# Another fixed order of TensorE in an attention iteration of a fused attention and expert kernel

## The chip, the cores and the metric

One core of one Trainium2 chip runs the whole program. The metric is the device time of one execution in microseconds (us). Three executions of the kernel before took 1117.29, 1118.50 and 1119.31 us; their median, 1118.5 us, is the time that is forecast against.

## What is computed

```python
# attention: 4 batches x 8 heads, 576 tokens, 64 columns a head
scores = q @ k.T / 8 + cum[:, None] - cum[None, :]   # cum = cumsum(log(f)), causal mask
attn = softmax(scores); x = attn @ v
# expert layer 1: 2304 tokens x 512, 8 experts, the best one of each token
logits = x @ w_gate + modality_bias[modality_id]
out = gate * (relu(x @ w1[e]) @ w2[e])
# layer 2: a rational function between two dense products
y = (P(h) / Q(h)) @ w_out      with h = out @ w_in
```

The change is in the first part alone, where the attention runs and the gate's logits are made from its result.

## The kernel before

The 32 heads are worked on in 16 pairs. Iteration p of the loop over pairs holds steps of several pairs at once, as a software pipeline: it turns q and k of pair p+2, finds the row maxima of pair p+1, makes the scores of pair p, multiplies the scores of pairs p-2 and p-1 with their values and makes the logits of pair p-2. There are 18 iterations; all steps are present in iterations 2 to 13.

Every operation is first recorded, with the tiles that it reads and writes. A planner (`Rec.flush`, L222) then orders the instructions of each engine: from a cost of each operation it simulates the engines, and an engine that becomes free takes, of the operations that are ready, the one with the best key; if one alone is ready, it takes that. The order of TensorE in the attention is the exception. While `nc.chained` is set, each TensorE operation is tied behind the one recorded before it, so TensorE follows the order of recording. That order is written out by hand in the string `ORDER` (L1445), read two characters at a time in the loop at L1527:

- M0 to M3 (`maxes`, L718): the scores of pair p+1, a quarter at a time, into a pair of PSUM banks; VectorE reduces them to row maxima. M1 is reduced in two pieces (896 and 128 columns), M2 in one of 576, M3 in one of 640.
- S0 to S3 (`scores`, L759): the scores of pair p, a quarter at a time, into a pair of banks; ScalarE takes the exponential from there, and GpSimd makes the low half of it.
- V (`values`, L790): the next chunk of 12 or 14 matmuls of the product with v; the digit is only a name. A pair has seven chunks: three for its first three blocks of tokens, four for the last two. The last three chunks of pair p-2 are V5, V6 and V7 of iteration p; then v0 opens pair p-1, and V1 to V4 are its first four. All chunks write one single PSUM bank ("pv"). Behind V3 and V7 VectorE divides what stands there by the sums in three instructions (a small TENSOR_SCALAR, a RECIPROCAL, and a TENSOR_TENSOR into x) and so empties the bank.
- L0, L1 (`logits`, L910): L0 turns x of pair p-2 in five transposes (three read the first three blocks of tokens, two the last two) into a pair of banks; ScalarE and VectorE split it in two halves. L1 multiplies these with the gate's weights, into the single bank "x". The stores of x to DRAM are recorded with L0.
- T0, T1 (`parts`, L671): T0 turns 512 tokens of q and k of pair p+2 in eight transposes into a pair of banks. `split` (L689) empties it: a copy on ScalarE makes the high half, then a subtraction on VectorE the low half, 1024 columns each. T1 does the same for the last 64 tokens in two transposes, by the bank "x" and 128 columns.
- m0 (`turned`, L748): turns the maxima of pair p+1, by the bank "x"; VectorE reduces them, and two DMAs put them into the tile that S0 of the next iteration reads.

The pairs of banks are a ring of three, taken in the order of recording by M, S, L0 and T0. So each of them waits until what stood three places before it has been read. The order before gives this: L0 takes the pair of M1, T0 that of S1, M3 that of M2, S2 that of L0, S3 that of T0. The bank "x" goes round m0, T1, L1.

```python
ORDER = "M0V5S0V6M1V7S1M2L0v0V1T0M3V2S2m0V3T1S3L1V4"
for x, g in zip(ORDER[::2], ORDER[1::2]):
    if x == "M" and p + 1 < NP:
        at.maxes(p + 1, int(g))
```

Of the kernel before, what the change touches and what calls it, by code (L numbers as in the profile page):

```python
# [1441 lines left out]
RW = (4, 3, 3)  # L1442
TW = 8
NR = (2, 2, 2, 2, 2)
ORDER = "M0V5S0V6M1V7S1M2L0v0V1T0M3V2S2m0V3T1S3L1V4"  # L1445
UP = {'conv': -2110000.0, 'conv2': -3000.0, 'early': 0, 'unit': -7000.0}


def program(tc, q, k, v, f, moe_modality_id, moe_w_gate, moe_modality_bias, moe_w1, moe_w2, moe2_w_in, moe2_w_out, moe2_a, moe2_b, out):
    nc = Rec(tc.nc)  # L1450
    with tc.manual_schedule(), ExitStack() as pools, tc.tile_pool(name="dr", bufs=1, space=DRAM) as dr:
# [64 lines left out]
        for p in range(NP + 2):  # L1516
# [7 lines left out]
            if p + 2 < NP:  # L1524
                at.prep(p + 2)
                t = at.parts(p + 2)
            for x, g in zip(ORDER[::2], ORDER[1::2]):  # L1527
                if x == "M" and p + 1 < NP:
# [85 lines left out]
```

## Time and profile before

| | us |
|---|---|
| median of three runs | 1118.5 |
| the profiled execution | 1123.07 |
| span of its instructions | 1121.4 |
| mean granted TensorE clock | 0.956 |
| TensorE busy | 1003.1 |
| VectorE busy | 854.4 |
| ScalarE busy | 651.3 |
| GpSimd busy | 405.4 |

The profiled execution took 1.7 us more than its span, and 0.4% more than the median. In the trace PE is TensorE, DVE VectorE, ACT ScalarE, POOL GpSimd, and SP the engine that issues most DMAs. Nearly all operations go through one helper, so they carry its line, L155; the groups of M and S carry L713. A step is told by its tiles and shapes: `pair<-keep,y` is L0, `pair<-keep,prep` T0, `one<-keep,prep` T1, `one<-keep,at` m0, `one<-y` L1, `one<-at` and `one<-at,old` V, and `pair<-f32r` M or S. In square brackets stands the idle time of the engine ahead of a row, and what ended it.

### The profile page before, as it was taken

The numbers are of one execution on the slowest core, as the hardware profiler recorded it, in microseconds if no ns is written. First come the engines' busy times: TensorE is split into PE (matmuls) and PEld (weight loads), VectorE is DVE, ScalarE is ACT, GpSimd is POOL, SyncE is SP. The second block draws the span as 40 slices with busy tenths as digits, with TensorE's granted clock in tenths as the row PEclk, the third lists the DMA queues.
The fourth block names the chain that finished last, engine by engine and source line by source line (L and its number), as shares of the span: only waits on it lengthen the run. The fifth ranks groups of instructions, "written<-read, shape, count | busy, mean of one in ns | idle before, by whom it ended". The sixth has DMA issues, their size and how long they took to land.

```text
span 1121.4 us, 22693 instructions
## 1 busy us (share of the span) xinstructions
PE 1003.1 (89%) x8246; PEld 853.2 (76%) x8246; DVE 854.4 (76%) x1557; ACT 651.3 (58%) x1034; POOL 405.4 (36%) x353
## 2 busy tenths in 40 slices
PE   3689988898746799999999999999999999999995
PEld 2577777776634578879888898889878887888793
DVE  5775756758788896787869767949769969979685
ACT  1465554465545675656567466637658667676472
POOL 9576675676742431223122121212222223121131
PEclk9999998898758699999999999999999999999999
DMA  7663333211478887301151543445354454553400
GB/s 180 166 172 86 105 73 82 51 45 47 99 233 220 268 270 238 83 1 39 48 160 46 153 134 102 142 132 151 114 163 140 119 182 132 156 154 105 123 1 19
DMA packets 157376, 138.28 MB, mean 123 GB/s; under 512 B 73392, under 2 KB 115664, under 8 KB 157264
## 3 DMA queue, kind: packets, MB, share of 16 engines
q1 hardware_dynamic: 152288, 123.63, 39.1%
q0 software_dynamic: 4640, 13.13, 3.7%
q8 instruction: 64, 1.05, 0.4%
q14 instruction: 48, 0.39, 0.1%
q10 hardware_dynamic: 336, 0.08, 0.0%
HBM read 120.38 MB, written 16.33 MB: 122 GB/s over the span
## 4 chain that ended last, share of the span: by engine, by line
PE 50%; DVE 22%; DMA 9%; issue 9%; ACT 4%; POOL 2%; SPq 2%; DVEq 0%; POOLq 0%; ACTq 0%
PE pair L155 31%; PE one L155 13%; DVE y L155 12%; PE pair L713 6%; DMA b<-in_moe_w_dram 4%; DVE at L155 4%; DVE b L155 4%; ACT y L155 3%; DVE keep L155 2%; ACT b L155 1%; SPq L155 1%; DVE f32r L155 1%; POOL f32r L155 1%; POOL y L155 1%; DMA ys<-b 1%
## 5 line engine op out<-in xcount | busy, mean ns | idle before, releaser
L155 DVE TENSOR_TENSOR b<-b,b 128x512 fp32r<-128x512 f32 x272 | 200.5, 746 | 67.6 <-ACT b L155 36.4
L155 PE MATMUL pair<-b,b 128*128 128x256 f32 (+1 forms) x1032 | 234.8, 329 | 16.5 <-DVE b L155 10.2
L155 ACT CAST b<-b 128x512 fp32r<-128x512 f32 x272 | 165.1, 618 | 124.4 <-PE one L155 46.1
L155 POOL TENSOR_TENSOR y<-y,y 128x512 f32<-128x512 f32 x72 | 107.3, 1491 | 302.4 <-ACT y L155 284.0
L155 PEld LDWEIGHTS pair<-b,b 128*128 128x128 f32 x1032 | 174.1, 198 | 50.2 <-DVE b L155 19.0
L155 PE MATMUL one<-b,b 128*128 128x512 f32 x552 | 181.1, 404 | 5.1 <-DVE b L155 3.3
L713 PE MATMUL pair<-f32r 64*128 64x288 f32 (+4 forms) x1152 | 128.6, 343 | 16.5 <-ACT f32r L155 6.8
L155 ACT ACTIVATE y<-y,keep 128x512 f32<-128x512 f32 x144 | 109.3, 769 | 36.1 <-POOL y L155 29.1
L155 POOL TENSOR_TENSOR old<-old,at 128x960 f16<-128x960 f32 (+1 forms) x64 | 109.6, 1724 | 46.6 <-ACT at L155 46.3
L155 DVE SCALAR_TENSOR_TENSOR y<-y,keep,y 128x512 f32<-128x512 f32 x144 | 116.9, 822 | 7.9 <-ACT y L155 4.6
L713 PEld LDWEIGHTS pair<-f32r 64*128 64x128 f32 x1152 | 94.6, 204 | 25.3 <-ACT f32r L155 7.3
L155 PE MATMUL pair<-f32r,y 128*128 128x512 f32 x378 | 110.9, 397 | 1.7 <-DVE y L155 1.6
L155 PEld LDWEIGHTS one<-b,b 128*128 128x128 f32 x552 | 95.7, 188 | 21.9 <-DVE b L155 6.8
L155 PE MATMUL pair<-y,f32r 128*128 128x256 f32 x624 | 103.8, 283 | 1.8 <-DVE y L155 1.8
L155 PEld LDWEIGHTS pair<-y,f32r 128*128 128x128 f32 x624 | 91.7, 188 | 9.3 <-DVE y L155 3.4
L155 ACT ACTIVATE old<-pair,keep 128x960 f32<-128x960 f32 (+1 forms) x64 | 59.4, 928 | 66.9 <-PE pair L713 63.9
L155 DVE TENSOR_REDUCE at<-pair 128x2 f32<-128x576 f32 (+1 forms) x96 | 66.2, 707 | 34.8 <-PE pair L713 30.6
L155 PE MATMUL pair<-at,y 128*128 128x512 f32 x270 | 90.1, 410 | 1.7 <-DVE y L155 1.4
L155 ACT ACTIVATE y<-y 128x512 f32<-128x512 f32 x104 | 66.8, 643 | 31.0 <-DMA y<-in_moe_w_in_dram 23.9
L155 PEld LDWEIGHTS pair<-f32r,y 128*128 128x128 f32 x378 | 67.8, 188 | 16.2 <-DVE y L155 4.1
L155 POOL DMA_INDIRECT keep<-xnat,keep x32 | 34.4, 1075 | 120.3 <-PE pair L155 50.9
L155 ACT ACTIVATE y<-pair,keep 128x512 f32<-128x512 f32 x70 | 54.3, 776 | 25.0 <-DVE y L155 20.2
(140 smaller groups left out, 1872.9 us busy)
## 6 DMA issues: line engine op xcount, KB each, us to landing
b<-in_moe_w_dram SPq DMA_DIRECT2D x272, 256.0 KB
y<-in_moe_w_in_dram SPq DMA_DIRECT2D x16, 512.0 KB
y<-in_moe_w_out_dram SPq DMA_DIRECT2D x16, 512.0 KB
ys<-b SPq DMA_DIRECT2D x25, 257.0 KB
y<-ys SPq DMA_DIRECT2D x18, 257.0 KB
prep<-in_v_dram SPq DMA_DIRECT2D x4, 1152.0 KB
prep<-in_q_dram SPq DMA_DIRECT2D x32, 128.0 KB
prep<-in_v_dram SPq DMA_DIRECT2D x32, 128.0 KB
```

The lines of the kernel that those rows point to most:

```text
L155: fn = lambda: getattr(getattr(s.nc, eng), name)(*(x() for x in ra), **{n: x() for n, x in rk.items()})
L713: T.matmul(o, lhsT=w, rhs=x, start=st, stop=sp, skip_group_check=True)
```

## The change

One string is replaced. L0 moves from between M2 and V1 to between V2 and S2, and so behind T0 and M3; T1 moves from between V3 and S3 to directly behind T0; V3 now stands ahead of m0. Since the ring of bank pairs follows the order of recording, its users change too: T0 now takes the pair of M1, M3 that of S1, L0 that of M2, S2 that of T0, and S3 that of M3. The bank "x" now goes round T1, m0, L1. No operation is added or removed, and the planner makes the order of the other engines anew.

```diff
-ORDER = "M0V5S0V6M1V7S1M2L0v0V1T0M3V2S2m0V3T1S3L1V4"
+ORDER = "M0V5S0V6M1V7S1M2v0V1T0T1M3V2L0S2V3m0S3L1V4"
```

## Rows read from the trace of the kernel before

**Rows 1.** The profile page: busy time of the engines, share of the span, instructions.
```profile
PE 1003.1 (89%) x8246; PEld 853.2 (76%) x8246; DVE 854.4 (76%) x1557; ACT 651.3 (58%) x1034; POOL 405.4 (36%) x353
```

**Rows 2.** Windows, 20 us of attention: length, busy time and instructions by engine, clock, DMA.
```profile
100.00:120.00 20.00, 19.00 (x334) 16.31 (x332) 12.13 (x33) 10.90 (x13) 11.84 (x10) 1.00 0.42 108
```

**Rows 3.** Timeline of PE, end of M2 to the next M0: start, length, engine, operation.
```profile
104.33 0.23 PE L713 MATMUL pair<-at 64*128 64x64 bf16 x4
104.61 0.55 PE L155 MATMUL pair<-keep,y 128*128 128x128 f32 x3
105.81 0.53 PE L155 MATMUL pair<-keep,y 128*128 128x128 f32 x2 [0.66 <-DVE y L155]
106.28 0.23 PE L155 MATMUL one<-at 128*128 128x65 f16 x2
...
106.65 1.07 PE L155 MATMUL pair<-keep,prep 128*128 128x128 f32 x8
107.65 0.56 PE L713 MATMUL pair<-f32r 64*128 64x320 f32 x4
...
108.22 0.29 PE L155 MATMUL one<-at 128*128 128x65 f16 x4
...
108.68 1.09 PE L713 MATMUL pair<-f32r 64*128 64x448 f32 x8
...
110.27 0.38 PE L155 MATMUL one<-keep,at 128*10 128x128 f32 x2
110.49 0.26 PE L155 MATMUL one<-at,old 128*128 128x65 f16 x3
...
111.16 0.27 PE L155 MATMUL one<-keep,prep 64*128 64x64 f32 x1
...
112.35 0.63 PE L155 MATMUL one<-y 128*128 128x8 f16 x15 [0.15 <-DVE f32r L155]
...
113.44 0.73 PE L713 MATMUL pair<-f32r 64*128 64x288 f32 x8
```

**Rows 4.** Waits of PE from 75 to 262 us: us in total, times, longest.
```profile
PE pair L155 <- DVE y L155: 7.0, 12, 0.7
...
PE pair L713 <- DMA f32r<-f32r: 1.1, 1, 1.1
```

**Rows 5.** Timeline of DVE in the iteration of rows 3.
```profile
104.67 0.76 DVE L155 TENSOR_REDUCE at<-pair 128x2 f32<-128x576 f32 x1
105.34 0.41 DVE L155 TENSOR_TENSOR y<-one,at 128x256 f32<-128x256 f32 x1
...
108.33 0.83 DVE L155 TENSOR_REDUCE at<-pair 128x2 f32<-128x640 f32 x1 [0.35 <-PE pair L713]
109.07 1.22 DVE L155 TENSOR_TENSOR f32r<-pair,f32r 128x1024 fp32r<-128x1024 f32 x1
```

**Rows 6.** Timeline of ACT in the same iteration.
```profile
107.76 1.01 ACT L155 CAST f32r<-pair 128x1024 fp32r<-128x1024 f32 x1
```

**Rows 7.** Timeline of all engines around 207 to 212 us.
```profile
207.51 3.05 DVE L155 TENSOR_TENSOR_SCAN keep<-keep 128x8 f32<-128x8 f32 x1
...
209.15 1.37 POOL L155 TENSOR_TENSOR at<-prep,at 128x640 f16<-128x640 f32 x1
...
211.34 0.59 PE L155 MATMUL one<-keep,at 128*10 128x128 f32 x2 [1.58 <-DVE at L155]
```

**Rows 8.** Timeline of PE in iteration 1, which also works out scales by the bank "x".
```profile
64.28 0.39 PE L155 MATMUL one<-at 96*128 96x4 f32 x2
65.51 0.38 PE L155 MATMUL one<-keep,at 128*10 128x128 f32 x2 [0.84 <-DVE at L155]
```

**Rows 9.** The chain that ended last, behind the attention: start, length, what.
```profile
312.02 6.05 DMA b<-in_moe_w_dram
```

**Rows 10.** Windows of PE: length, busy time (instructions), granted clock, DMA share, GB/s.
```profile
200.00:211.30 11.30, 8.91 (x145) 1.00 0.33 79
211.40:221.50 10.10, 9.69 (x118) 0.50 0.20 41
```

## The prediction

> **What bounds the kernel now.** I read the page first: TensorE is busy 89% of the span, no other engine over 76% [rows 1]. Then the windows, for the stage that the change touches: in 20 us of attention TensorE works 19.0, VectorE, ScalarE and GpSimd about 11 to 12 each, at the full clock [rows 2]. So the attention goes at TensorE's pace, in the order that the string gives, and what can be won or lost is the time in which TensorE, in its fixed order, stands waiting. Third, the timeline of one iteration [rows 3], 14.60 us long by the M0 at its end and the same step before. It is regular: the wait inside L0 for VectorE's y occurs 12 times from 75 to 262 us, 7.0 us in all, never over 0.7 [rows 4], once in each of the 12 iterations that have all steps. Last, what VectorE does meanwhile [rows 5].
>
> The iteration waits at these places. M2 ends at 104.33 + 0.23 = 104.56. L0 begins at 104.61; its last two transposes wait 0.66 for the division of V7's bank, which VectorE ends at 105.34 + 0.41 = 105.75, and V1, into that same bank, follows at 106.28. T1 stands 0.21 late: V3 begins at 110.49, and a chunk takes 0.46 (V2 at 108.22, S2 at 108.68), so it ends at 110.95, and T1 starts at 111.16, as the bank "x" is still held by m0. L1 waits 0.15 for T1's split [rows 3, 5].
>
> **The change, part by part.** It moves instructions and removes none, so TensorE's work stays, and each step is costed by its waits. All is worked out on the iteration of rows 3.
>
> *L0 away from M2.* V1 now stands directly behind M2. It writes the bank that the division empties, so it cannot start before what L0's second part waited for: 105.81, the same moment. The planner has no reason to move the division: everything up to M2 is in the old order, and VectorE takes M2's reduction (104.67) ahead of it because that is ready while the division still waits for its reciprocal. So the stall from 104.56 is 1.25 us, where it was 0.05 and 0.66, and L0's first three transposes no longer lie in it.
>
> *From V1 to S2.* By the starts in rows 3: V1 takes 0.37 (106.28 to 106.65), T0 1.00, M3 0.57, V2 0.46. T0 does eight transposes of 128 columns in 1.00, or 0.125 each; so T1's two of 64 columns cost 0.13, and L0 in one piece 4 x 0.125 + 0.06 = 0.56. Without a wait S2 would come 1.00 + 0.13 + 0.57 + 0.46 + 0.56 = 2.72 behind T0's start.
>
> *S2's pair of banks.* This is the larger price. S2 used to take the pair that L0 left; now it takes T0's, two TensorE steps after T1. That pair is free when VectorE ends the subtraction: 109.07 + 1.22 = 110.29, or 3.64 behind T0's start at 106.65 [rows 3, 5]. Between ScalarE's copy (ending 108.77, [rows 6]) and it lies M3's reduction, which is ready first. In the new order M3 starts 0.13 later, so I take 3.64 + 0.13 + 0.05 (from the division's end to L0's start) = 3.82. S2 waits 3.82 - 2.72 = 1.10. If the planner puts the subtraction first, it starts soon behind the copy, 2.2 after T0's start, and S2 comes at 2.2 + 1.22 + 0.05 = 3.5. These are the two ends; I take 3.82, since the reduction is the one that is ready first.
>
> *S2 to the next M0.* 113.44 - 108.68 = 4.76 before. T1's 0.13, its 0.21 and L1's 0.15 go: 4.27. V3 ahead of m0 leaves TensorE's work as it is. What covers m0's chain to S0 (reduction, SP's two DMAs) shrinks by V3 and T1's part, about 1 us; S0 waited for these DMAs in one iteration of twelve, 1.1 us [rows 4]. Bounds 0 to 1 an iteration; I take 0.5 in all.
>
> *The other instructions moved.* SP's loads that T1 frees are recorded earlier and are due an iteration later; the stores of x wait for the division alone. L0's split (ScalarE, VectorE) ends long before L1, behind S2, V3, m0 and S3. T0's pair was reduced ahead of 104.67, M3's and L0's before they come. I put these at nothing; T0's and S2's waits are the cover, and if it failed the price would be one split, under 1 us.
>
> *Sum of one iteration.* V1 at 105.81 as L0's second part before. S2 then at 105.81 + 0.37 + 3.82 = 110.00, where it was 108.68: +1.32. Less 0.49 behind it: **+0.83 us**, 12 times: +10.0.
>
> *Single iterations.* In one, VectorE is held by a scan of 8 columns for 3.05 us (207.51 to 210.56), and m0 behind it stalls 1.58 [rows 7]; without the stall m0 would stand at 209.76, and M3's reduction 1.94 ahead of it (108.33 to 110.27, [rows 3, 5]), at 207.8; it came behind the scan, 2.7 later. Now S2, which stands before m0, would wait that much longer, and m0 no more: 2.7 - 1.6 = +1.1 (0 to 2.7). In iteration 1 the bank "x" is used by the scales until past 64.28, and m0 waits 0.84 for it [rows 8]; T1 now comes to that bank 2.6 us before m0 did (107.65 to 110.27 in rows 3). The planner can hasten the scales: 0 to +2.6, I take +0.6.
>
> [...]
>
> *Behind the attention* the chain runs into the loads of expert weights, one at 312.02 [rows 9], whose buffers the attention has held until then, but conversion of other weights stands there as well. Between half and all of the delay passes; I take all: 10.0 + 1.1 + 0.6 + 0.5 = **+12.2** (low end +6). The profiled execution's 1123.07 us, span 1121.4 and 1.7 around it, becomes 1135.3. It was 4.6 over the median; carried to that, **1130.7 us**.
>
> **The rivals.**
> - *Half clock* (chance 0.20). The stall of 1.58 us at 209.8 ends at 211.34; the clock was 1.00 up to 211.3 and then 0.50, the lower of its two levels, from 211.4 to 221.5 [rows 7, 10]. The waits of 0.66 went without a fall. A stall of 1.25 lies between, and a second of 1.10 follows some 4 us later. A fall costs about half of the 9.69 us of work done under it, 4.8, less the S2 wait that it hides, 1.1: 3.7. In every second iteration that is 6 x 3.7 = 22: 1152. [...]
> - *The subtraction first on VectorE* (0.10). S2 at 105.81 + 0.37 + 3.5 = 109.68, +1.00 - 0.49 = +0.5 an iteration, +6: 1124.5.
> - *Faster: the planner serves TensorE's waits first* (0.15). If it puts the division ahead of M2's reduction, V1 comes 0.67 earlier, at 105.14 (105.34 - 104.67); with the subtraction also first, S2 is at 105.14 + 0.37 + 3.5 = 109.01, +0.33 - 0.49 = -0.16, 12 times -2. It decides from the point at which both are moved; one alone isn't enough. If the accident at 207 us then finds another place as well, its 1.58 and half of 9.69 go, 6.4 more: 1110. Against it: both reductions are ready first in rows 5.
> - *Nothing measurable* (0.05): the waits cancel, or the plan behind the attention gives them back: 1118.5.
>
> That the string has no effect can't be: TensorE's operations are tied in its order.
>
> **How the numbers follow.** Likeliest, 0.50: 1130.7, its own range 1124 to 1136. A difference under 0.2%, 2.2 us, is about what a measurement of this kernel can't tell from none. Slower holds 0.50 + 0.20 + 0.10, less 0.03 for their lower edge: 0.77; within 0.2% 0.08; faster 0.15. The range 1113 to 1152 leaves out half of the faster case and the upper half of the half-clock one, 0.17 together.
>
> **What would show it.** Right: in the profile after, V1's first row behind M2 waits some 1.25 us for VectorE's y, S2's first row about 1.1 for its subtraction into `f32r`, T1 and L1 wait for nothing, the period is about 15.4 us, and the attention ends 10 to 12 us later. Wrong: S2 starts without a wait (another pair of banks, or the subtraction early), VectorE takes the division ahead of M2's reduction, or the expert stage begins no later. If the clock is 0.50 in iterations that had 1.00, the first rival holds.

## The result, and the profile after

The kernel after takes **1129.5 us** in the median of four executions (1128.22 to 1137.28), beside 1118.9 of the kernel before on the same chip: a ratio of **1.0124, 95% interval 1.0086 to 1.0162**. This ratio and those in the table of the experiments are estimates from the fast runs of both kernels, and not the quotient of the two medians (here 1.0095). Its profiled execution took 1130.75 us with a span of 1129.0. The forecast was 1130.7.

| us | before | after | |
|---|---|---|---|
| T0 of iteration 2 starts | 77.23 | 77.59 | +0.4 |
| from there to T0 of iteration 13, 11 periods | 178.4 | 185.1 | +6.7 |
| from there to the start of the last L1 | 56.7 | 58.5 | +1.8 |
| behind that | 809.1 | 807.8 | -1.3 |
| span | 1121.4 | 1129.0 | +7.6 |

T0 itself stands nearer to M2 in the kernel after (it starts 1.61 us behind M2's end, before 2.09), so its start is not the same point of an iteration in both. Counted at M0, the kernel after is 1.7 us late in iteration 3 and 9.4 in iteration 14; it is 9.0 late at the start of the last L1 and 7.5 at its end.

The page of after, which answers to [rows 1], has TensorE's and VectorE's busy time within 1%: no work came or went.

```profile
PE 994.2 (88%) x8246; PEld 847.5 (75%) x8246; DVE 860.8 (76%) x1557; ACT 652.8 (58%) x1034; POOL 404.9 (36%) x353
```

The timeline of TensorE of after, end of M2 to the next M0, answers to [rows 3]:

```profile
108.42 0.24 PE L713 MATMUL pair<-at 64*128 64x64 bf16 x4
109.91 0.22 PE L155 MATMUL one<-at 128*128 128x65 f16 x2 [1.25 <-DVE y L155]
...
110.27 1.07 PE L155 MATMUL pair<-keep,prep 128*128 128x128 f32 x8
111.27 0.27 PE L155 MATMUL one<-keep,prep 64*128 64x64 f32 x1
...
111.42 0.54 PE L713 MATMUL pair<-f32r 64*128 64x320 f32 x3
...
111.96 0.29 PE L155 MATMUL one<-at 128*128 128x65 f16 x4
...
112.33 0.83 PE L155 MATMUL pair<-keep,y 128*128 128x128 f32 x5
114.16 1.08 PE L713 MATMUL pair<-f32r 64*128 64x448 f32 x8 [0.99 <-DVE f32r L155]
...
116.11 0.38 PE L155 MATMUL one<-keep,at 128*10 128x128 f32 x2
...
117.28 0.64 PE L155 MATMUL one<-y 128*128 128x8 f16 x15
...
118.39 0.73 PE L713 MATMUL pair<-f32r 64*128 64x288 f32 x8
```

V1 stands directly behind M2 and waits 1.25. S2 waits 0.99. T1, m0 and L1 follow without a bracket. VectorE in the same iteration (answers to [rows 5]):

```profile
108.77 0.76 DVE L155 TENSOR_REDUCE at<-pair 128x2 f32<-128x576 f32 x1
109.45 0.41 DVE L155 TENSOR_TENSOR y<-one,at 128x256 f32<-128x256 f32 x1
112.14 0.83 DVE L155 TENSOR_REDUCE at<-pair 128x2 f32<-128x640 f32 x1 [2.28 <-PE pair L713]
112.89 1.22 DVE L155 TENSOR_TENSOR f32r<-pair,f32r 128x1024 fp32r<-128x1024 f32 x1
```

The division ends at 109.45 + 0.41 = 109.86, just ahead of V1's 109.91. T0's subtraction stands behind M3's reduction and ends at 114.11, just ahead of S2's 114.16. TensorE's waits from 75 to 262 us, to be read beside [rows 4] (us in total, times, longest), show both as a thing of nearly every iteration. This stretch holds 11 places of each; S2 waits at all of them, V1 at 10:

```profile
PE pair L713 <- DVE f32r L155: 14.1, 11, 4.3
PE one L155 <- DVE y L155: 12.4, 10, 1.5
PE pair L713 <- DMA f32r<-f32r: 2.2, 3, 1.1
```

What this does to a period, T0 to T0, must be read among iterations with the same work, and windows over each show which are: length, busy time of TensorE (instructions), granted clock, DMA share, GB/s. Before:

```profile
106.70:122.60 15.90, 14.90 (x260) 1.00 0.56 152
152.40:173.30 20.90, 14.79 (x233) 0.93 0.32 66
206.10:226.30 20.20, 17.51 (x233) 0.75 0.27 62
241.10:255.60 14.50, 13.51 (x233) 1.00 0.08 22
```

After:

```profile
110.30:127.00 16.70, 14.46 (x260) 1.00 0.52 145
142.40:159.30 16.90, 13.56 (x233) 1.00 0.33 73
159.40:176.20 16.80, 13.65 (x233) 1.00 0.38 73
209.10:231.70 22.60, 17.06 (x231) 0.77 0.26 55
247.30:262.60 15.30, 13.06 (x232) 1.00 0.09 22
```

An undisturbed iteration of 231 to 236 instructions took 14.60 to 14.62 before and 15.44 to 15.47 after. (A window also counts the few matmuls that reach into it; by their starts they are 230.) One of 260 carries 26 more matmuls and took 15.96, now 16.78. Both are 0.8 us longer. Those of 243 took 15.08 before, and 15.29 and 15.99 after. The others hold single events: a longer stall (up to 4.61 us before, 4.29 after), a wait for a DMA (up to 1.1 us in both), a fall of the clock (means of 0.93, 0.75 and 0.77 in the windows above).

### The profile page after: what moved, and what is told of

It reads as the page before. It is cut to its first block, busy times and chain, and to the rows that moved or that the text cites. A ratio compares the mean times of both kernels' runs of the same rounds, so it can differ in the third digit from the quotient of the medians.

```text
span 1129.0 us, 22712 instructions
## 1 busy us (share of the span) xinstructions
PE 994.2 (88%) x8246; PEld 847.5 (75%) x8246; DVE 860.8 (76%) x1557; ACT 652.8 (58%) x1034; POOL 404.9 (36%) x353
## 4 chain that ended last, share of the span: by engine, by line
PE 37%; DVE 15%; issue 6%; DMA 4%; ACT 4%; POOL 1%; SPq 1%; DVEq 0%; POOLq 0%; ACTq 0%
PE pair L155 29%; DVE y L155 11%; PE one L155 8%; DVE b L155 4%; ACT y L155 3%; DMA ys<-b 2%; DMA b<-in_moe_w_dram 1%; ACT b L155 1%; DMA y<-ys 1%; DMA y<-in_moe_w_in_dram 1%; POOL y L155 1%; DMA out_dram<-y,keep 0%; SPq L1358 0%; DVEq L155 0%; SPq L1182 0%
## 5 line engine op out<-in xcount | busy, mean ns | idle before, releaser
L155 PE MATMUL pair<-b,b 128*128 128x256 f32 (+1 forms) x1032 | 234.1, 326 | 20.8 <-ACT b L155 10.6
L155 ACT CAST b<-b 128x512 fp32r<-128x512 f32 x272 | 165.0, 618 | 124.8 <-PE one L155 47.1
L155 POOL TENSOR_TENSOR old<-old,at 128x960 f16<-128x960 f32 (+1 forms) x64 | 112.3, 1764 | 56.3 <-ACT at L155 56.0
L155 ACT ACTIVATE old<-pair,keep 128x960 f32<-128x960 f32 (+1 forms) x64 | 59.0, 925 | 61.9 <-PE pair L713 57.1
L155 PE MATMUL one<-at 128*128 128x65 f16 (+1 forms) x968 | 60.6, 202 | 25.4 <-DVE y L155 21.5
```

The source lines that it names most:

```text
L155: fn = lambda: getattr(getattr(s.nc, eng), name)(*(x() for x in ra), **{n: x() for n, x in rk.items()})
```

## The experiments

All were compared with the kernel before, executed on the same chip. The table holds the profiled execution of each, in us: the period of an undisturbed iteration with 230 to 236 instructions (the range of the shortest two or more); the start of T0 of iteration 2; the 11 periods behind it; from there to the start of the last L1; behind that; the span. The row of before is its one profiled execution. The last column is the ratio to the kernel before, with its interval. Where an order moves T0 within the iteration, the columns "T0" and "to L1" hold that move too; the text then counts from M0 of iteration 14, the last M0, which starts at 262.4 before and at 271.7 after. Each kernel is described below.

| | period | T0 | 11 periods | to L1 | behind | span | ratio |
|---|---|---|---|---|---|---|---|
| before | 14.60-14.62 | 77.2 | 178.4 | 56.7 | 809.1 | 1121.4 | 1 |
| after | 15.44-15.47 | 77.6 | 185.1 | 58.5 | 807.8 | 1129.0 | 1.0124 [1.0086, 1.0162] |
| L0 only | 15.84-15.86 | 77.8 | 190.2 | 58.3 | 810.6 | 1136.8 | 1.0126 [1.0054, 1.0197] |
| L0 stays | 14.20-14.30 | 81.0 | 172.4 | 57.7 | 811.9 | 1123.0 | 1.0047 [1.0009, 1.0085] |
| T1 only | 14.19-14.21 | 80.9 | 171.7 | 61.9 | 814.4 | 1128.9 | 1.0074 [1.0043, 1.0104] |
| V1 ahead of L0 | 14.91-15.07 | 79.1 | 183.8 | 60.9 | 810.3 | 1134.1 | 1.0064 [1.0023, 1.0106] |
| M3 ahead of T0 | 14.50-14.53 | 80.2 | 181.9 | 64.4 | 810.4 | 1136.9 | 1.0110 [1.0036, 1.0184] |
| T0 ahead of V1 | 13.43-13.64 | 79.3 | 162.4 | 62.5 | 808.7 | 1112.9 | 1.0019 [0.9981, 1.0056] |
| T0 ahead of M2 | 13.91-13.95 | 78.7 | 170.0 | 63.4 | 813.1 | 1125.1 | 1.0009 [0.9975, 1.0042] |
| m0 ahead of V3 | 15.45-15.47 | 79.9 | 186.8 | 59.3 | 813.7 | 1139.7 | 1.0176 [1.0126, 1.0225] |
| before, four `mt` | 14.59-14.62 | 76.5 | 174.4 | 60.8 | 808.9 | 1120.6 | 0.9980 [0.9944, 1.0016] |
| after, four `mt` | 15.45-15.47 | 81.0 | 191.0 | 58.7 | 814.2 | 1144.8 | 1.0178 [1.0124, 1.0232] |
| T0 first, m0, four `mt` | 13.42-13.66 | 77.6 | 165.0 | 63.8 | 813.8 | 1120.1 | 0.9990 [0.9956, 1.0023] |
| after again | 15.46-15.47 | 79.7 | 184.6 | 58.0 | 812.1 | 1134.4 | 1.0140 [1.0101, 1.0178] |

### The change taken apart

**L0 only.** L0 moves as in the change; T1, m0 and V3 stay.

```diff
-ORDER = "M0V5S0V6M1V7S1M2L0v0V1T0M3V2S2m0V3T1S3L1V4"
+ORDER = "M0V5S0V6M1V7S1M2v0V1T0M3V2L0S2m0V3T1S3L1V4"
```

> L0 alone is moved, to behind V2; T1 and V3 stay where the kernel before has them. Theory of the two waits (V1, directly behind M2, waits for the division that empties its bank; S2, now the third user of a bank pair behind T0, waits for T0's subtraction): V1 waits about 1.25 us and S2 about 1.1 us in each of 12 iterations, T1 and L1 keep their 0.2 and 0.15; S2 comes 0.37 + 3.64 + 0.05 = 4.06 us behind V1's start, where it was 2.87 behind the same moment, so the period is 14.6 + 1.2 = 15.8 us and the time about 1118.9 + 14 = 1133 us, more than the changed kernel's 1129.5. Rival, T1 directly behind T0 is what costs (it delays M3, its reduction and T0's subtraction): then this kernel stays near 1119 us and its S2 waits little. Rival, the cost is the new plan of the other engines and not the waits: the period stays near 14.6 us and the time anywhere within some 4 us of 1119.

The median was 1140.35 us, beside 1125.55 for the kernel before. Waits of TensorE from 75 to 272 us:

```profile
PE pair L713 <- DVE f32r L155: 15.5, 12, 4.3
PE one L155 <- DVE y L155: 15.2, 12, 1.4
```

Both waits are there without T1, and the period, 15.85, is even 0.4 longer than after's: T1 stands late again. So the loss comes with L0's move alone, and T1's move gives some of it back.

**L0 stays.** The other half of the change: T1 behind T0, V3 ahead of m0.

```diff
-ORDER = "M0V5S0V6M1V7S1M2L0v0V1T0M3V2S2m0V3T1S3L1V4"
+ORDER = "M0V5S0V6M1V7S1M2L0v0V1T0T1M3V2S2V3m0S3L1V4"
```

> The changed order with L0 alone put back between M2 and V1: T1 directly behind T0 and V3 ahead of m0 as in the change. Theory of the two waits: the ring is the old one (S2 takes L0's bank pair), L0's first three transposes lie again in the wait behind M2, and T1's 0.21 and L1's 0.15 us of waiting are gone; M3 comes 0.13 us later. Period 14.6 - 0.36 = 14.2 us, time about 1118.9 - 4 = 1115 us. Rival, T1 behind T0 is what costs: the period is above 14.6 us and the time near 1125 us or more. Rival, the plan: no change of the period, the time within some 4 us of 1119.

Waits of TensorE from 75 to 262 us, its first two lines:

```profile
PE pair L155 <- DVE y L155: 8.0, 12, 1.1
PE pair L713 <- DMA f32r<-f32r: 2.6, 4, 1.6
```

S2's wait for `f32r` every iteration is gone and the period fell to 14.2 to 14.3, as the theory of the two waits has it. The time did not follow: 1128.47 us, slower than before, where a gain was expected. The 11 periods gave 6.0 us, but T0 of iteration 2 came 3.8 later, and 1.0 and 2.8 went behind. S0 waits for m0's DMAs four times.

**T1 only.** T1 behind T0, with V3 left behind m0.

```diff
-ORDER = "M0V5S0V6M1V7S1M2L0v0V1T0M3V2S2m0V3T1S3L1V4"
+ORDER = "M0V5S0V6M1V7S1M2L0v0V1T0T1M3V2S2m0V3S3L1V4"
```

> The order before with T1 alone moved directly behind T0; m0 stays ahead of V3 and L0 between M2 and V1. Theory: T1's 0.2 and L1's 0.15 us of waiting go, period 14.2 to 14.3 us where the kernel before has 14.6, S0 waits for m0's DMAs no more than before (the run with L0 alone put back, which has V3 ahead of m0, waited 2.6); the last T0 comes about 4 us earlier. The tail behind it gave back half of such gains in two runs (they ended 0.6 and 8.1 us earlier after a lead of 4.7 and 13.9), so 2 to 4 us under the kernel before, 0.2 to 0.4%. Rival, that T1 behind T0 costs: period above 14.6.

The period is 14.2 again, and again the time is higher, 1131.95 us beside 1122.79, with 3.7 us lost ahead of iteration 2 and 5.2 and 5.3 behind the 11 periods. Moving T1 shortens the iteration; what eats it stands outside it.

**V1 ahead of L0.** From the kernel before, V1 alone moves ahead of L0, so that V1 stands directly behind M2 but the users of the bank pairs stay as they were.

```diff
-ORDER = "M0V5S0V6M1V7S1M2L0v0V1T0M3V2S2m0V3T1S3L1V4"
+ORDER = "M0V5S0V6M1V7S1M2v0V1L0T0M3V2S2m0V3T1S3L1V4"
```

> The order before with v0 and V1 put ahead of L0 and nothing else: the ring of bank pairs is as before, so S2 still takes L0's pair. It prices the first wait alone. Theory of the two waits: V1 waits about 1.25 us behind M2 and L0 follows without a wait; lost is what the first three transposes did inside that wait, 0.45 us an iteration: period 15.05 us, time about 1118.9 + 12 x 0.45 = 1124 us, S2 with no wait or a short one. Rivals (T1's place, or the plan): period 14.6 us, time within some 3 us of 1119.

Waits of TensorE from 75 to 265 us, first line:

```profile
PE one L155 <- DVE y L155: 14.4, 11, 1.6
```

V1 waits its 1.25, S2 has no wait for `f32r`, and the period is 14.9 to 15.07. So the first wait comes from V1's place and is worth 0.3 to 0.45 us, and the second one doesn't come from it. The time was 1133.96 us beside 1125.55, 8.4 us more where 5.4 was expected; the interval holds both.

### The two waits taken away

**M3 ahead of T0.** From the kernel after. Now T0 takes the pair of S1, L0 that of M2, and S2 that of M3, which is reduced early.

```diff
-ORDER = "M0V5S0V6M1V7S1M2v0V1T0T1M3V2L0S2V3m0S3L1V4"
+ORDER = "M0V5S0V6M1V7S1M2v0V1M3T0T1V2L0S2V3m0S3L1V4"
```

> The changed order with M3 moved ahead of T0 and T1, so that the third user behind T0 is S3 and S2 takes M3's bank pair. It takes the second wait away and leaves the first. Theory of the two waits: V1 still waits about 1.25 us, S2 starts without a wait, V1 to S2 is 0.37 + 0.57 + 1.00 + 0.13 + 0.46 + 0.56 = 3.09 us where the changed kernel needs about 4.25; period 15.45 - 1.1 = 14.3 us, time near 1116 us, about 13 us under the changed kernel. Rival, the plan or T1's place: the time stays near 1129 us, as T1 is still directly behind T0 and L0 behind V2.

TensorE in one iteration, T0 to L0 and S2:

```profile
110.03 1.09 PE L155 MATMUL pair<-keep,prep 128*128 128x128 f32 x8
...
111.69 0.84 PE L155 MATMUL pair<-keep,y 128*128 128x128 f32 x5
112.27 1.13 PE L713 MATMUL pair<-f32r 64*128 64x448 f32 x8
```

S2 starts without a bracket, and the period falls by 0.95 to 14.5: S2's wait is the bank pair of T0, shown by giving it another one. Again the time stayed high, 1137.74 us, where some 3 us under the kernel before was expected. The waits from 75 to 262 us hold new single ones in their place:

```profile
PE one L155 <- DVE y L155: 16.4, 12, 3.5
PE pair L713 <- DMA f32r<-f32r: 3.5, 4, 2.7
```

A wait of 3.5 ahead of V1 at 222.59 and one of 2.7 ahead of S0 at 168.33 are each about what three iterations gain. M0 of iteration 14 comes 3.0 us earlier than after's, and the way from there to the last L1 is 8.2 longer.

**T0 ahead of V1.** From the kernel after: T0 and T1 fill the time in which V1 waits for the division. The pairs go M2, T0, M3, L0, S2, so S2 still takes T0's, but V1 lies between.

```diff
-ORDER = "M0V5S0V6M1V7S1M2v0V1T0T1M3V2L0S2V3m0S3L1V4"
+ORDER = "M0V5S0V6M1V7S1M2T0T1v0V1M3V2L0S2V3m0S3L1V4"
```

> The changed order with T0 and T1 put between M2 and V1: T0's 1.00 and T1's 0.13 us lie in the wait for the division, and T0's subtraction has 1.5 us more before S2, which still takes T0's bank pair. Theory of the two waits: V1 waits 0.1 us instead of 1.25, S2 between 0 and 0.9 (by whether the subtraction or M3's reduction comes first on VectorE): period 13.6 to 14.3 us where the kernel before has 14.6, so 4 to 12 us under the kernel before if the single stalls stay as they are, and 14 to 22 under the changed kernel. Rival, that L0 behind V2 or T1 directly behind T0 is what costs: both are so here, and the period stays near 15.4 us.

TensorE in one iteration: T0, T1 and V1.

```profile
93.86 1.10 PE L155 MATMUL pair<-keep,prep 128*128 128x128 f32 x8
94.88 0.34 PE L155 MATMUL one<-keep,prep 64*128 64x64 f32 x2
95.39 0.22 PE L155 MATMUL one<-at 128*128 128x65 f16 x2 [0.18 <-DVE y L155]
```

V1's wait is 0.18 here (4.6 us in the 12 iterations) and S2 starts without one (it waits twice from 75 to 245 us, 2.0 in all). The shortest period, 13.43, is 1.2 us under that of the kernel before. The 11 periods together are 16 us shorter, 13 of it by the regular period. The profiled execution took 1114.59 us, the shortest of the 12, but their median is 1122.76 beside 1124.91: no difference that these runs can tell, where 4 to 12 us were expected. The last M0 comes 11.7 us earlier than before's, the last L1 only 8.1. Windows from the last M0 to the last L1 hold the same number of matmuls in both: length, busy time of TensorE, its weight loads, VectorE, ScalarE and GpSimd (instructions), clock, DMA share, GB/s. Before, then this kernel:

```profile
262.40:312.30 49.90, 38.46 (x564) 32.20 (x562) 39.44 (x78) 26.69 (x39) 35.20 (x24) 0.76 0.35 88
```

```profile
250.70:304.10 53.40, 38.73 (x564) 33.30 (x561) 38.50 (x79) 25.50 (x38) 35.04 (x25) 0.67 0.47 104
```

The stretch is 3.5 us longer, at a lower clock. TensorE's waits for VectorE's `y` in it are 12.0 us in seven, and 8.8 in seven for the kernel before.

**T0 ahead of M2.** One step further.

```diff
-ORDER = "M0V5S0V6M1V7S1M2v0V1T0T1M3V2L0S2V3m0S3L1V4"
+ORDER = "M0V5S0V6M1V7S1T0T1M2v0V1M3V2L0S2V3m0S3L1V4"
```

> The changed order with T0 and T1 put between S1 and M2: T0 takes S0's bank pair, M2 that of M1, L0 that of T0 and S2 that of M2. Theory of the two waits: V1 comes behind M2 with the division done (VectorE has no M2 reduction before it), S2 without a wait, and L0 waits some 0.6 us for T0's subtraction: period about 13.7 us, 8 to 11 us under the kernel before if the single stalls stay. Rival, that L0's place or T1's costs: period near 15.4 us.

The period is 13.9; L0 now waits 0.49 for T0's subtraction. The time, 1126.11 us, is the same as before's within the interval.

### Other suspects

**m0 ahead of V3.** After's S0 waits 2.2 us for m0's DMAs in three iterations, 1.1 before. If m0's later place did that, it should go.

```diff
-ORDER = "M0V5S0V6M1V7S1M2v0V1T0T1M3V2L0S2V3m0S3L1V4"
+ORDER = "M0V5S0V6M1V7S1M2v0V1T0T1M3V2L0S2m0V3S3L1V4"
```

> The changed order with m0 put back ahead of V3. It tells what V3 ahead of m0 costs by the two DMAs that m0's result takes to the next S0: in the changed kernel S0 waits 2.2 us for them in all from 75 to 262 us (three iterations), before 1.1. Theory: V1's 1.25 and S2's 0.99 us stay, the regular period stays at 15.45 us, and S0's waits fall to about 1 us: 1 to 2 us under the changed kernel at most, and still slower than before by about 1%. Rival, that m0's place is the main cost: the period falls below 15 us and the time to near the kernel before.

These waits are 2.3 us in four iterations, so m0's place is not what makes them, and 1142.11 us is no gain.

**Before, four `mt`.** In the kernel before, one iteration takes 20.99 us, and this is behind it: GpSimd scatters a tile `mt` into a table in DRAM, and VectorE, which writes the same tile for the next batch, waits for it. VectorE, then TensorE, in the kernel before:

```profile
166.95 2.59 DVE L155 TENSOR_SCALAR keep<-keep 128x5 int32<-128x5 int32 x1 [5.78 <-DMA table<-keep]
...
170.58 0.28 DVE L155 TENSOR_REDUCE at<-pair 128x2 f32<-128x128 f32 x1
```

```profile
170.91 0.90 PE L155 MATMUL pair<-keep,y 128*128 128x128 f32 x3 [4.61 <-DVE at L155]
```

TensorE stands at L0 for 4.61 us, until VectorE ends M1's reduction at 170.86, since L0 takes the bank pair of M1. The clock is 0.50 from 170.4 to 177.2. The experiment gives every batch a tile of its own.

```diff
-        mt = t([P, NB, 2], "mt")
+        mt = t([P, NB, 2], f"mt{b}")
```

> The kernel before, with a tile of its own for each batch in place of the one tile mt, from which the table's scatters read. In the trace before, an instruction that writes mt for the next batch waits 5.8 us on VectorE for the last scatter, and TensorE behind it stalls 4.6 us at 171 us and then runs at half clock from 170.4 to 177.2. Theory (the change's two waits cost about 0.85 us in each of 12 iterations, and the changed kernel's plan happened to drop this one accident): without the reuse the stall and the half clock there are gone, the step from the 8th to the 9th T0 falls from 21 to about 15 us, and the attention ends 5 to 7 us earlier: about 0.5% under the kernel before. Rival (the stall has another cause, or is paid anyhow): no change beyond 2 us.

The wait of VectorE is gone, and the longest of L0's waits is 0.8. The iteration still takes 19.32 us: S0 waits 1.4 for m0's DMA instead, and the clock falls:

```profile
161.60:168.50 6.90, 6.90 (x72) 0.51 0.26 53
```

The last T0 comes 4.7 us earlier and the last L1 0.6; the median is 1121.93 us, no difference to 1124.91, where 0.5% was expected.

**After, four `mt`.** The same line in the kernel after.

> The changed kernel with a tile of its own for each batch in place of the one tile mt. In its trace no TensorE wait over 1.5 us hangs on that tile, so the theory expects no change beyond 2 us: about 1.2% above the kernel before, and about 1.7% above the kernel before with the same edit, which is the price of the two waits without that accident (12 x 0.85 = 10 us, and 5 to 9 us more at single iterations). Rival (the reuse is paid in both kernels alike): this one gains as much as the kernel before does, and their distance stays near 10 us.

1145.69 us, a ratio of 1.0178, where no change, and so about 1.012, was expected; its interval begins at 1.0124. The regular period is after's, 15.45 to 15.47; the single waits fall otherwise (S0 for DMAs 4.1 us, one of them 3.1). This one line, which changes no order of TensorE, moved the 11 periods of before by -4.0 and those of after by +5.9.

**T0 first, m0, four `mt`.** The shortest regular period, with m0 ahead of V3 and a tile for each batch, as a candidate for a kernel that beats both.

```diff
-ORDER = "M0V5S0V6M1V7S1M2v0V1T0T1M3V2L0S2V3m0S3L1V4"
+ORDER = "M0V5S0V6M1V7S1M2T0T1v0V1M3V2L0S2m0V3S3L1V4"
-        mt = t([P, NB, 2], "mt")
+        mt = t([P, NB, 2], f"mt{b}")
```

> T0 and T1 between M2 and V1, L0 behind V2, m0 ahead of V3, and a tile of its own for each batch in place of mt. Theory: V1's and S2's waits are covered (period about 13.5 us), S0's waits for m0's DMAs are below 1.5 us in all, no stall hangs on mt: the last T0 comes about 14 us earlier than before. If the tail behind it gives half back, as in two runs, the time is 7 us under the kernel before (0.6%); if it passes all, 14 us (1.2%). Rival, that the time of the attention is set by its single stalls and not by the regular waits: no gain beyond 2 us.

The shortest periods are 13.4 to 13.7, the last M0 comes 8.0 us earlier than before's, and the time is 1122.68 us beside 1122.79. From the last M0 to the last L1 2.1 us are given back, and 4.7 behind that.

**After again.** The kernel after unchanged, on another chip.

> The changed kernel itself once more, beside the kernel before on the same chip as the variants, where single executions of the kernel before spread over 1116 to 1136 us. Theory: each attention iteration pays 0.85 us more, as in its first profile (V1 waits 1.25, S2 0.99, period 15.45), whatever the single stalls do in an execution: 1.0 to 1.8% above the kernel before, with the regular period the same to 0.05 us and the rest of the difference in single stalls (S0 on DMAs, falls of the clock) that differ between the two profiles. Rival, that the first comparison of four executions each was a matter of its plan's luck on that day: within 0.5% of the kernel before.

1136.98 us beside 1124.0, a ratio of 1.0140; 13.0 us more. The period and both waits are the same (1.25, 0.98 and once 4.3). Behind the last L1 this execution took 812.1 us, the first one 807.8.

## Why the prediction was right, point by point

**V1 behind M2: 1.25 us forecast, 1.25 measured.** The planner left M2's reduction ahead of the division, as in [rows 5], so V1 found the bank at the same moment as L0's second part had. V1 ahead of L0 shows this wait alone.

**S2 and T0's bank pair: S2 3.82 behind T0's start forecast, 3.89 measured; wait 1.10 forecast, 0.99 measured.** The moment is set by M3's reduction and the subtraction, and these came as costed. The wait is what is left of it. TensorE's way there was forecast at 2.72; L0 starts at 112.33, 2.06 behind T0, and takes 0.58 where nothing waits behind it (M3 ahead of T0: 111.69 to 112.27), 0.56 by my step. That makes 2.64 and a delay of 3.89 - 2.64 = 1.25, of which the row counts 0.99 as idle, from the modelled end of L0's row on. V2 is the term that was mis-sized, 0.37 (111.96 to 112.33) instead of 0.46. It cost nothing, since the wait takes up what it leaves. M3 ahead of T0 shows the cause.

**Behind S2: 4.27 forecast, 4.23 measured** (114.16 to 118.39). T1 and L1 wait for nothing. L0 stays shows this part alone: 0.3 to 0.4 us less a period.

**One iteration: +0.83 forecast, +0.82 to +0.87 measured.** The parts add up by the shortest periods of the experiments: T1's move -0.4, V1's place +0.3 (from L0 stays, 14.2, to M3 ahead of T0, 14.5), S2's pair +0.95 (from there to after).

**The scan iteration: +0.83 and +1.1 forecast, +2.44 measured** (20.32 to 22.76). S2 took the stall from m0, as said. VectorE, GpSimd and TensorE of after:

```profile
210.38 3.35 DVE L155 TENSOR_TENSOR keep<-keep 128x8 f32<-128x8 f32 x1
...
211.10 1.28 POOL L155 TENSOR_TENSOR old<-old,at 128x576 f16<-128x576 f32 x1
212.33 1.36 POOL L155 TENSOR_TENSOR at<-prep,at 128x640 f16<-128x640 f32 x1
...
214.19 0.82 DVE L155 TENSOR_REDUCE at<-pair 128x2 f32<-128x640 f32 x1
214.92 1.22 DVE L155 TENSOR_TENSOR f32r<-pair,f32r 128x1024 fp32r<-128x1024 f32 x1
...
216.19 1.12 PE L713 MATMUL pair<-f32r 64*128 64x448 f32 x4 [4.29 <-DVE f32r L155]
```

The long instruction of 8 columns is another one of the same chain now, 3.35 us instead of 3.05; M3's reduction and the subtraction queue behind it, and S2 waits 4.29, where 1.10 + 2.7 = 3.8 was the sum.

**Iteration 1: 0 to +2.6 forecast, +0.6 taken, +0.4 measured** in T0 of iteration 2. The planner did hasten the scales, as thought possible: the same matmuls that stood at 64.28 in [rows 8] now come at 60.52, and wait there.

```profile
60.52 0.39 PE L155 MATMUL one<-at 96*128 96x4 f32 x2 [2.52 <-DVE at L155]
```

T0's nearer place hides part of it: at M2's end of iteration 2 the delay is 0.8. That it was so little is luck of one execution: the second profile of the same kernel, after again, has that T0 2.5 us later than before's, at 79.7. L0 stays and T1 only have the same wait, 2.54 and 2.92, and are 3.7 to 3.8 us late at T0 of iteration 2.

**m0's DMAs: +0.5 forecast, +1.1 measured** in the waits of TensorE.

**What I had not seen.** The step of the sum that failed is the one that isn't in it: I let every other single event of before stand. The scatter that held VectorE 5.78 us and TensorE 4.61 in before still holds VectorE in after, for 3.20 us, but no wait of TensorE hangs on that:

```profile
170.61 1.05 DVE L155 TENSOR_SCALAR keep<-keep 128x5 int32<-128x5 int32 x1 [3.20 <-DMA table<-keep]
```

The two periods around it fell from 20.99 + 17.67 to 16.92 + 16.76, 6.6 us less than the forecast's regular addition would give (38.66 + 1.66 against 33.68). So in the 11 periods: 9.4 for the regular part (11 x 0.85), 1.6 more in the scan's, -6.6 here, and a remainder of 2.3, in which S0's longer waits and a fall of the clock behind V1 (below) lie, together 6.7, where the forecast's terms come to 10.7 (9.1 + 1.1 + 0.5). The profiled span grew by 7.6 against 12.2, while the medians differ by 10.6 on one chip and 13.0 on another. That the median was met within 1.2 us is therefore partly chance; the mechanism and its regular size are what the runs show. In time, all five comparisons of kernels with both waits (after twice, L0 only, m0 ahead of V3, after with four `mt`) lie at 1.0124 to 1.0178, and all eight of kernels that have only one of them regularly, or none, at 0.9980 to 1.0110. Among these eight the time does not follow the period: M3 ahead of T0, at 14.5 us, is at 1.0110. So how much of the time is the regular waits' and how much the single events' rests on the sums of the profiled executions above; the times alone don't separate the two.

**Behind the attention: all of the delay passes.** The attention ended 9.0 us later by the start of the last L1, 7.5 by its end, where the forecast had 10 to 12. The span behind that start was 807.8 and 812.1 in the two profiled executions of after, 809.1 before (behind the end of L1 806.3 and 810.5, before 806.1), so what the attention lost wasn't made up. For gains it isn't so simple, and that the forecast did not ask: the kernels with shorter periods lose 2 to 4 us between the last M0 and the last L1 (T0 ahead of V1, T0 ahead of M2, T0 first), and up to 5 behind. In that stretch of T0 ahead of V1 TensorE waits longer for VectorE's `y` (12.0 us, before 8.8), and its clock is lower, 0.67 instead of 0.76. Why VectorE is later there, and how much of this is the plan and how much one execution, stays open.

**The rivals.** *Half clock*: after's windows from 142.4 to 176.2 and from 247.3 hold both waits in each iteration at a granted clock of 1.00, so a wait of 1.25 and one of 0.99 some 4 us later didn't lower it there. The clock records of before and after hold 1.00 and 0.50 alone; in the 11 periods of after it fell to 0.50 twice, and both times behind a longer wait: behind V1's 1.48 at 92.91, and behind S2's 4.29.

```profile
92.90:96.30 3.40, 3.39 (x28) 0.50 0.45 121
215.90:225.90 10.00, 9.71 (x107) 0.50 0.10 22
```

But the length of the wait alone doesn't tell. In after again V1 waits the same 1.48 us in the same iteration, and the clock stays at 1.00. TensorE, then the window behind it:

```profile
95.00 0.22 PE L155 MATMUL one<-at 128*128 128x65 f16 x2 [1.48 <-DVE y L155]
```

```profile
95.00:98.50 3.50, 3.25 (x47) 1.00 0.63 158
```

*The subtraction first* and *the planner serves TensorE's waits first* fell with VectorE's order, which is that of [rows 5]. *Nothing measurable* is excluded by both intervals of after.

## What to carry to other kernels

With an engine in a fixed order and buffers in a ring, moving one step gives every later step another predecessor in the ring: write down the new partner of each and the moment at which that partner is read empty, and the wait can be worked out (here 1.25 and 1.10 us forecast, 1.25 and 0.99 measured). A step that was filling another one's wait (here three transposes of L0) is missed when it leaves, and the best filler found was a step whose result is wanted late (T0). But a better regular iteration is not a better kernel: where a planner sets the other engines' order, the edits here also dealt single stalls and clock falls anew, some us either way (four `mt` moved the 11 periods by -4.0 in before and +5.9 in after), and the next bound must be known before a gain of 16 us in a stage is counted.

## What the runs showed of the hardware

- A VectorE TENSOR_TENSOR on 8 columns took 3.35 us in after (210.38 to 213.73) and ended within 0.04 of the end of a GpSimd TENSOR_TENSOR (213.69); the scan of 3.05 us in [rows 7] ended 0.04 from one as well (210.56 and 210.52). With no GpSimd TENSOR_TENSOR beside them, a TENSOR_TENSOR of that shape took 0.15 us (212.34 in before) and the scan 0.17 (210.16 in after). In both cases two GpSimd instructions stood close behind each other (211.10 to 213.69; 207.91 to 210.52 in before), and VectorE's, which began before the second, ended with the second. GpSimd's own took 1.28 and 1.36 us in after and 1.29 and 1.37 in before, where they take 1.27 to 1.30 and 1.35 to 1.38 in the other iterations, so the whole delay stands in VectorE's instruction. The subtraction of T0, with one input in PSUM, took 1.22 us (112.89 to 114.11) with a GpSimd TENSOR_TENSOR from 112.45 to 113.82 beside it, and 1.21 to 1.22 in the other iterations. What holds the one up and not the other isn't shown.
- The executions of one kernel differ by more than the change: 29 executions of the kernel before on one chip took 1117.1 to 1131.4 us. Their time goes with their mean granted TensorE clock (0.951 in the longest, 0.959 in the shortest; correlation -0.82, 8 us for each 0.01). On two other chips the correlation is weaker, -0.59 (23 executions) and -0.73 (11), with 5 to 6 us for each 0.01, so the falls of the clock vary with the time; that they are its cause isn't shown. Two executions with a profile can't settle a gain of 0.5%.
- V1's waits of 1.25 us in after's windows from 142.4 to 176.2 and from 247.3 passed at a granted clock of 1.00; of its two waits of 1.48 us, one stood ahead of a fall to 0.50 (after, 92.91) and one did not (after again, 95.00, with 1.00 behind it).
